# Attention scores of four 32-row heads in one PSUM tile, in place of two zero-padded pairs

## The chip, the cores and the metric

The kernel runs on one core of one Trainium2 chip. The metric is the device time of one execution in microseconds (us). Engines are named as the profile names them: PE is TensorE (PEld its weight loads), ACT is ScalarE, DVE is VectorE, POOL is GpSimd. Matmuls write into PSUM buffers; "FFN" is the feed-forward half of the block, "PV" the product of probabilities and values.

## The reference

One transformer block with its whole backward pass: 2048 positions, width 448, 16 heads of 28 channels, FFN width 1792, bf16.

```python
xn = layernorm(x)
q, k, v = split_heads(xn @ wqkv)                        # 16 heads of 28
p = softmax(einsum("bhqd,bhkd->bhqk", q, k) * 28**-0.5)
A = merge_heads(einsum("bhqk,bhkd->bhqd", p, v)) @ wo
B = (silu(xn @ w_gate) * (xn @ w_up)) @ w_down
out = x + A + B
# outputs: out, and the gradients of x, wqkv, wo, w_gate, w_up, w_down for a given grad_out
```

## The kernel before

A head's 28 channels are padded to 32 rows, so that four heads fill the 128 partitions; G = 4 such groups. For the score matmuls the kernel keeps a second copy of Q and K in DRAM (`PAIR_d`) in which a head occupies 64 rows, 32 of them zeros. Two heads lie in the two 64-row halves of PE and run side by side. Their scores form one tile of two PSUM banks, and two such tiles are in flight. Forward FFN units and weight-gradient units (`pfe`) are woven into the same loop, so that PE has other work while ACT computes exponentials.

```python
ps_u = pf.enter_context(tc.tile_pool(name="pf_psu", bufs=2, space=PSUM))   # FFN banks
...
ework = p3.enter_context(tc.tile_pool(name="p3_e", bufs=5))
ps_s = p3.enter_context(tc.tile_pool(name="p3_pss", bufs=2, space=PSUM))   # 2 tiles of 2 banks
ps_o = p3.enter_context(tc.tile_pool(name="p3_pso", bufs=1, space=PSUM))
ps_t = p3.enter_context(tc.tile_pool(name="p3_pst", bufs=1, space=PSUM))
for g in range(G):
    ...                                              # loads of qk (PAIR_d) and Vsp
    for qc in range(4):                              # 512 queries
        for kt in range(NT):                         # 16 blocks of 128 keys: 256 turns in all
            eTs = []
            for hp in range(2):
                s_ps = ps_s.tile([P, 2, 512], FP32, name="s_ps")
                for j in range(2):
                    nc.tensor.matmul(s_ps[:, j, :],
                        lhsT=KT2[hp][64*j:64*(j+1), kt*P:(kt+1)*P],
                        rhs=QT2[hp][64*j:64*(j+1), qsl],
                        start=True, stop=True, tile_position=(64*j, 0))
                eT = ework.tile([P, 2, 512], BF16, name="eT")
                nc.scalar.activation(out=eT[:], in_=s_ps[:], func=ACT.Exp, scale=SCALE)
                eTs.append(eT)
            if prev is not None:
                pv_quad(*prev)                       # four PV matmuls of the turn before
            prev = (kt, eTs)
            ...                                      # 56 ffn_unit and up to 168 pfe_unit over 256 turns
```

One weight-gradient step goes from PE to DVE and back to PE:

```python
pt = ps_u.tile([P, 4, P], BF16, name="ffn_ps")
for j in range(4):
    nc.tensor.transpose(pt[:, j, :], srcT[:, t*P:(t+1)*P], ident_bf[:])    # t = t4*4 + j
sp = ewk.tile([P, 4, P], BF16, name="ffn_sp")
nc.vector.tensor_copy(out=sp[:], in_=pt[:])
acc_ps = ps_u.tile([P, 512], FP32, name="ffn_ps")
for j in range(4):
    nc.tensor.matmul(acc_ps[:], lhsT=sp[:, j, :], rhs=rhs_sp[:, t, :], start=(j == 0), stop=(j == 3))
```

The builder sorts each engine's instructions again, so the order on PE is not that of the source; but once built it is fixed.

The softmax here doesn't subtract the row's maximum and nothing guards it: scores larger than these inputs give would overflow.

## Time and profile before

| | before |
|---|---|
| time, median of the first 3 runs | 2243 us (2233 to 2254) |
| first score matmul at | 118.8 us |
| attention forward, first score to last PV | 727 us, mean granted clock 0.96, PE busy 648 |
| tail, last PV to first output matmul | 166 us |
| output, attention backward, last gradients | 1237 us |

The lines that carry this stand in the prediction, whose forward and tail are cut within 1.1 us of these landmarks. Two more, from the page's list of costly groups (line, engine, operation, tiles, shapes, count, busy us, mean ns of one, idle before it and its main releaser):

```profile
L377 ACT ACTIVATE eT<-s_ps 128x1024 bf16<-128x1024 f32 x512 | 494.2, 1026 | 183.5 <-PE s_ps L372 170.1
L372 PE MATMUL s_ps<-qk 64*128 64x512 bf16 x1024 | 207.9, 389 | 38.8 <-ACT eT L377 32.2
```

The exponentials keep ACT busy for 494 us and the 1024 score matmuls PE for 208. ACT waits long for PE and PE briefly for ACT, so PE is the fuller of the two.

### The profile page before, as it was taken

Reading aid. Unit: us, or ns where it says so; the run is one execution under the profiler, and the core shown is the slowest. Engines: PE = TensorE matmul, PEld = TensorE weight load, DVE = VectorE, ACT = ScalarE, POOL = GpSimd, SP = SyncE. Lnnn points to the kernel's source line nnn. Section 1 sums busy time; section 2 is a strip of 40 time slices with the busy share of each in tenths; the row PEclk is TensorE's granted clock in tenths of the full one; section 3 lists DMA queues with packets and bytes.
Section 4 is the critical chain, followed back from the end, with each engine's and each line's share of the span. In section 5 each row is a group of like instructions: output and inputs, shape, how many; then the busy total and the mean of one; then the engine's idle time right before and its main releaser. Section 6 shows DMA issues by size and latency. Waiting matters only on the chain.

```text
span 2249.0 us, 30338 instructions
## 1 busy us (share of the span) xinstructions
PE 1827.5 (81%) x11579; PEld 685.4 (30%) x11672; DVE 1404.1 (62%) x2141; ACT 1086.5 (48%) x1167; POOL 25.9 (1%) x19
## 2 busy tenths in 40 slices
PE   3779989979989996569728888888888888875998
PEld 2433333333333332224302222222222222223554
DVE  4545546555555555532728788889798888874344
ACT  2167757757767770000016566656566666650100
POOL 2000000000000000000000000000000000001000
PEclk9999989989989998759858788879699979887999
DMA  5931131131121111152198887887887888787263
GB/s 200 292 110 61 63 110 61 63 109 63 55 106 63 47 46 49 61 189 95 36 338 178 155 166 170 169 164 166 158 173 164 165 171 174 150 157 229 88 202 110
DMA packets 658009, 299.56 MB, mean 133 GB/s; under 512 B 568072, under 2 KB 632712, under 8 KB 654792
## 3 DMA queue, kind: packets, MB, share of 16 engines
q1 hardware_dynamic: 632256, 252.16, 46.2%
q10 hardware_dynamic: 25608, 45.46, 6.2%
q8 instruction: 92, 1.51, 0.3%
q14 instruction: 53, 0.43, 0.1%
HBM read 99.74 MB, written 63.57 MB: 73 GB/s over the span
## 4 chain that ended last, share of the span: by engine, by line
PE 55%; DMA 18%; DVE 11%; ACT 10%; issue 5%; SPq 0%; ACTq 0%; another core or an unknown queue 0%; DVEq 0%
DMA dsT<-ds_sb 8%; PE ffn_ps L295 8%; PE dq_ps L601 7%; PE s_ps L372 5%; ACT e_sb L549 5%; PE sd_ps L530 4%; ACT eT L377 4%; DVE ds_sb L557 4%; PE o_ps L359 4%; PE sd_ps L541 4%; PE acc L572 3%; DMA srcT<-hT_d 2%; PE ffn_ps L235 2%; PE g_ps L726 2%; PE g_ps L724 2%
## 5 line engine op out<-in xcount | busy, mean ns | idle before, releaser
L557 DVE TENSOR_TENSOR ds_sb<-sd_ps,e_sb 128x1024 bf16<-128x1024 f32 x512 | 611.1, 1220 | 133.4 <-ACT e_sb L549 40.0
L549 ACT ACTIVATE e_sb<-sd_ps 128x1024 bf16<-128x1024 f32 x512 | 510.4, 1022 | 362.5 <-PE sd_ps L541 243.0
L377 ACT ACTIVATE eT<-s_ps 128x1024 bf16<-128x1024 f32 x512 | 494.2, 1026 | 183.5 <-PE s_ps L372 170.1
L530 PE MATMUL sd_ps<-bw_all 32*128 32x512 bf16 x1024 | 224.3, 431 | 57.1 <-DVE ds_sb L557 20.9
L601 PE MATMUL dq_ps<-dsT,sp_all 128*32 128x512 bf16 x1024 | 211.4, 464 | 71.6 <-DMA dsT<-ds_sb 56.3
L541 PE MATMUL sd_ps<-bw_all 32*128 32x512 bf16 x1024 | 225.0, 430 | 48.0 <-ACT e_sb L549 42.5
L372 PE MATMUL s_ps<-qk 64*128 64x512 bf16 x1024 | 207.9, 389 | 38.8 <-ACT eT L377 32.2
L572 PE MATMUL acc<-e_sb,sp_all 128*32 128x512 bf16 x1024 | 233.8, 442 | 0.3 <-DVE dkv_all L586 0.2
L579 PE MATMUL acc<-ds_sb,sp_all 128*32 128x512 bf16 x1024 | 230.0, 443 | 0.9 <-DVE ds_sb L557 0.9
L359 PE MATMUL o_ps<-eT,Vsp 128*32 128x512 bf16 x1024 | 166.8, 392 | 4.5 <-ACT eT L377 3.5
L295 PE MATMUL ffn_ps<-xn_sp,ffn_sp 128*128 128x512 bf16 x411 | 123.7, 421 | 22.3 <-DVE ffn_sp L291 18.0
L530 PEld LDWEIGHTS <-bw_all 32*128 32x128 bf16 x1024 | 57.5, 93 | 252.1 <-issue 245.9
L300 DVE TENSOR_TENSOR dwacc<-ffn_ps,dwacc 128x512 f32<-128x512 f32 x84 | 58.1, 691 | 119.3 <-PE ffn_ps L295 119.3
L541 PEld LDWEIGHTS <-bw_all 32*128 32x128 bf16 x1024 | 76.1, 93 | 148.0 <-issue 141.8
L601 PEld LDWEIGHTS <-sp_all 128*32 128x32 bf16 x1024 | 62.1, 107 | 148.1 <-issue 117.8
L291 DVE COPY ffn_sp<-ffn_ps 128x512 bf16<-128x512 bf16 x168 | 70.1, 417 | 52.6 <-PE ffn_ps L289 51.5
L372 PEld LDWEIGHTS <-qk 64*128 64x128 bf16 x1024 | 56.1, 93 | 143.9 <-issue 128.7
L289 PE MATMUL ffn_ps<-ident_bf,srcT 128*128 128x128 bf16 x672 | 73.8, 239 | 31.7 <-DMA srcT<-hT_d 17.6
L238 ACT ACTIVATE t_sb<-ffn_ps 128x512 f32<-128x512 f32 x56 | 33.5, 598 | 134.6 <-PE ffn_ps L235 134.4
L295 PEld LDWEIGHTS <-ffn_sp 128*128 128x128 bf16 x672 | 56.5, 104 | 122.8 <-DVE ffn_sp L291 59.0
L609 DVE TENSOR_TENSOR dq_acc<-dq_ps,dq_acc 64x512 f32<-64x512 f32 x96 | 65.9, 686 | 34.2 <-PE dq_ps L601 32.8
L726 PE MATMUL g_ps<-wuT_sb,duT_c 128*128 128x448 bf16 x224 | 80.1, 357 | 3.7 <-DMA duT_c<-duT_d 3.7
(137 smaller groups left out, 1886.3 us busy)
## 6 DMA issues: line engine op xcount, KB each, us to landing
qk<-PAIR_d SPq DMA_DIRECT2D x8, 1024.0 KB
dsT<-ds_sb SPq DMA_TRANSPOSE x512
hT_d<-hT SPq DMA_DIRECT2D x14, 512.0 KB
duT_d<-duT SPq DMA_DIRECT2D x14, 512.0 KB
srcT<-hT_d SPq DMA_DIRECT2D x14, 512.0 KB
daT_d<-daT SPq DMA_DIRECT2D x14, 512.0 KB
srcT<-daT_d SPq DMA_DIRECT2D x14, 512.0 KB
srcT<-duT_d SPq DMA_DIRECT2D x14, 512.0 KB
```

The lines of the kernel that those rows point to most:

```text
L295: nc.tensor.matmul(acc_ps[:], lhsT=sp[:, j, :], rhs=rhs_sp[:, t, :], start=(j == 0), stop=(j == 3))
L359: nc.tensor.matmul(o_ps[HP * hh:HP * (hh + 1), :], lhsT=Vsp[:, kt, HP * hh:HP * (hh + 1)], rhs=eTs[hp][:, j, :], start=(kt == 0), stop=(kt ...
L372: nc.tensor.matmul(s_ps[:, j, :], lhsT=KT2[hp][64 * j:64 * (j + 1), kt * P:(kt + 1) * P], rhs=QT2[hp][64 * j:64 * (j + 1), qsl], start=Tru ...
L377: nc.scalar.activation(out=eT[:], in_=s_ps[:], func=ACT.Exp, scale=SCALE)
L530: nc.tensor.matmul(s_ps[:, j, :], lhsT=QD[HP * j:HP * (j + 1), qt * P:(qt + 1) * P], rhs=KV[HP * j:HP * (j + 1), ksl], start=True, stop=Tr ...
L541: nc.tensor.matmul(dp_ps[:, j, :], lhsT=QD[64 + HP * j:64 + HP * (j + 1), qt * P:(qt + 1) * P], rhs=KV[64 + HP * j:64 + HP * (j + 1), ksl] ...
L549: nc.scalar.activation(out=e_sb[:], in_=s_ps[:], func=ACT.Exp, scale=SCALE)
L557: nc.vector.tensor_tensor(out=ds_sb[:], in0=dp_ps[:], in1=e_sb[:], op=ALU.mult)
L572: nc.tensor.matmul(acc[HP * j:HP * (j + 1), :], lhsT=dOlsp[:, qt, HP * hh:HP * (hh + 1)], rhs=e_sb[:, j, :], start=(qt == 0), stop=(qt == ...
L579: nc.tensor.matmul(acc[64 + HP * j:64 + HP * (j + 1), :], lhsT=Qsp[:, qt, HP * hh:HP * (hh + 1)], rhs=ds_sb[:, j, :], start=(qt == 0), sto ...
L601: nc.tensor.matmul(dq_ps[HP * hh:HP * (hh + 1), :], lhsT=Ksp[:, kc * 4 + kt, HP * hh:HP * (hh + 1)], rhs=dsT[:, j, kt, :], start=(kt == 0) ...
L726: nc.tensor.matmul(g_ps[:, :D], lhsT=duT_c[:, fc, tsl], rhs=wuT_sb[:, fc, :], start=(i == 0), stop=(i == n_mm - 1)); i += 1
```

## The change

The intent: four heads of 32 rows need no zero padding, four score matmuls run side by side in place of two and two, the padded copy of Q and K (and 16 stores of zeros) goes, and one exponential covers four heads. The score tile grows to four banks, so only one fits where two of two banks stood.

```diff
-    PAIR_d = dram.tile([G, 2, P, 2, S], BF16)
+    QK32_d = dram.tile([G, P, 2, S], BF16)
...                                       (memset of a zero tile and 16 stores of it removed)
-                    for hh in range(4):
-                        nc.sync.dma_start(out=PAIR_d[g, hh // 2, 64 * (hh % 2):64 * (hh % 2) + 32, tq, :],
-                                          in_=xT[HP * hh:HP * (hh + 1), :])
+                    nc.sync.dma_start(out=QK32_d[g, :, tq, :], in_=xT[:])
...
-        ework = p3.enter_context(tc.tile_pool(name="p3_e", bufs=5))
+        ework = p3.enter_context(tc.tile_pool(name="p3_e", bufs=3))
-        ps_s = p3.enter_context(tc.tile_pool(name="p3_pss", bufs=2, space=PSUM))
+        ps_s = p3.enter_context(tc.tile_pool(name="p3_pss", bufs=1, space=PSUM))
...                                       (two loads of 1 MB a group become one; pv_quad reads eT[:, hh, :])
-                    for hp in range(2):
-                        s_ps = ps_s.tile([P, 2, 512], FP32, name="s_ps")
-                        for j in range(2):
-                            nc.tensor.matmul(s_ps[:, j, :],
-                                             lhsT=KT2[hp][64 * j:64 * (j + 1), kt * P:(kt + 1) * P],
-                                             rhs=QT2[hp][64 * j:64 * (j + 1), qsl],
-                                             start=True, stop=True, tile_position=(64 * j, 0))
-                        eT = ework.tile([P, 2, 512], BF16, name="eT")
-                        nc.scalar.activation(out=eT[:], in_=s_ps[:], func=ACT.Exp, scale=SCALE)
-                        eTs.append(eT)
+                    s_ps = ps_s.tile([P, 4, 512], FP32, name="s_ps")
+                    for hh in range(4):
+                        nc.tensor.matmul(s_ps[:, hh, :],
+                                         lhsT=KT[HP * hh:HP * (hh + 1), kt * P:(kt + 1) * P],
+                                         rhs=QT[HP * hh:HP * (hh + 1), qsl],
+                                         start=True, stop=True, tile_position=(HP * hh, 0))
+                    eTs = ework.tile([P, 4, 512], BF16, name="eT")
+                    nc.scalar.activation(out=eTs[:], in_=s_ps[:], func=ACT.Exp, scale=SCALE)
```

More of the change, by code (lines that the diff above doesn't have):

```diff
@@ L82 @@
     nc.vector.memset(eps_t[:], EPS)
-    with tc.tile_pool(name="zpool", bufs=1) as zpool:
-        ztile = zpool.tile([P, 2, S], BF16)
-        nc.gpsimd.memset(ztile[:], 0.0)
-        for g in range(G):
-            for hp in range(2):
-                eng = nc.sync if (g + hp) % 2 == 0 else nc.scalar
-                eng.dma_start(out=PAIR_d[g, hp, 32:64], in_=ztile[32:64])
-                eng.dma_start(out=PAIR_d[g, hp, 96:128], in_=ztile[96:128])
     xn_sp = persist.tile([P, NT, DP_], BF16)
@@ L342 @@
         for g in range(G):
-            QT2, KT2 = [], []
-            for hp in range(2):
-                qk = inp.tile([P, 2, S], BF16, name=f"qk{hp}")
-                nc.sync.dma_start(out=qk[:], in_=PAIR_d[g, hp])
-                QT2.append(qk[:, 0, :])
-                KT2.append(qk[:, 1, :])
+            qk = inp.tile([P, 2, S], BF16, name="qk")
+            nc.sync.dma_start(out=qk[:], in_=QK32_d[g])
+            QT, KT = qk[:, 0, :], qk[:, 1, :]
             Vsp = inp.tile([P, NT, P], BF16, name="Vsp")
@@ L353, with pv_quad @@
                 o_ps = ps_o.tile([P, 512], FP32, name="o_ps")
-                def pv_quad(kt, eTs):
-                    for hp in range(2):
-                        for j in range(2):
-                            hh = 2 * hp + j
-                            nc.tensor.matmul(o_ps[HP * hh:HP * (hh + 1), :],
-                                             lhsT=Vsp[:, kt, HP * hh:HP * (hh + 1)],
-                                             rhs=eTs[hp][:, j, :],
-                                             start=(kt == 0), stop=(kt == NT - 1),
-                                             tile_position=(0, HP * hh),
-                                             skip_group_check=True)
+                def pv_quad(kt, eT):
+                    for hh in range(4):
+                        nc.tensor.matmul(o_ps[HP * hh:HP * (hh + 1), :],
+                                         lhsT=Vsp[:, kt, HP * hh:HP * (hh + 1)],
+                                         rhs=eT[:, hh, :],
+                                         start=(kt == 0), stop=(kt == NT - 1),
+                                         tile_position=(0, HP * hh),
+                                         skip_group_check=True)
@@ L366 @@
                 prev = None
                 for kt in range(NT):
-                    eTs = []
-                    for hp in range(2):
-                        s_ps = ps_s.tile([P, 2, 512], FP32, name="s_ps")
-                        for j in range(2):
-                            nc.tensor.matmul(s_ps[:, j, :],
-                                             lhsT=KT2[hp][64 * j:64 * (j + 1), kt * P:(kt + 1) * P],
-                                             rhs=QT2[hp][64 * j:64 * (j + 1), qsl],
-                                             start=True, stop=True, tile_position=(64 * j, 0))
-                        eT = ework.tile([P, 2, 512], BF16, name="eT")
-                        nc.scalar.activation(out=eT[:], in_=s_ps[:], func=ACT.Exp, scale=SCALE)
-                        eTs.append(eT)
+                    s_ps = ps_s.tile([P, 4, 512], FP32, name="s_ps")
@@ new lines @@
+                    for hh in range(4):
+                        nc.tensor.matmul(s_ps[:, hh, :],
[4 more added lines that the diff above has]
+                    nc.scalar.activation(out=eTs[:], in_=s_ps[:], func=ACT.Exp, scale=SCALE)
```

## The prediction

> **What bounds the kernel now.** I read the busy rows over 40 slices of the page first, then the busy time of each engine in six stretches that I cut at landmarks of the timeline, then the waits and the timeline inside the stretches that the change touches.
>
> The busy tenths in 40 slices:
>
> ```profile
> PE   3779989979989996569728888888888888875998
> ACT  2167757757767770000016566656566666650100
> PEclk9999989989989998759858788879699979887999
> DMA  5931131131121111152198887887887888787263
> ```
>
> ScalarE (ACT) works in slices 2 to 15 and again from slice 21 on: the attention forward and the attention backward. The diff touches only the first of these, and the projection stage ahead of it. Between them lies a stretch where ACT is at 0 and the granted clock sinks to 0.5. The stretches in numbers (PE, weight load, VectorE, ACT, GpSimd busy us, clock, DMA share, GB/s):
>
> ```profile
> 0.00:118.80 118.80, 66.78 (x514) 40.30 (x523) 62.87 (x151) 19.74 (x34) 14.04 (x14) 1.00 0.78 250
> 118.80:846.50 727.70, 648.10 (x3809) 245.35 (x3875) 402.73 (x771) 522.60 (x561) 3.12 (x2) 0.96 0.21 72
> 846.50:1011.00 164.50, 107.49 (x434) 45.00 (x441) 78.49 (x144) 4.78 (x8) 0.00 (x0) 0.69 0.29 99
> ```
>
> The first is loads and projections (DMA 78% busy), the second the attention forward with the FFN woven into it (PE 89% busy, ACT 72%), the third a tail: FFN work that did not fit beside the attention, at a mean clock of 0.69. The rest (1238 us) is output, attention backward and last gradients.
>
> Inside the forward, the waits:
>
> ```profile
> ACT eT L377 <- PE s_ps L372: 170.1, 209, 11.1
> PE s_ps L372 <- ACT eT L377: 32.2, 101, 1.0
> ```
>
> ACT waits for scores 170 us, PE for the exponentials only 32 us: mostly PE's turn order bounds the forward. The PE timeline shows what a turn costs (start, duration):
>
> ```profile
> 150.37 0.39 PE L372 MATMUL s_ps<-qk 64*128 64x512 bf16 x2
> 150.69 0.39 PE L359 MATMUL o_ps<-eT,Vsp 128*32 128x512 bf16 x2
> 151.01 0.39 PE L372 MATMUL s_ps<-qk 64*128 64x512 bf16 x2
> ...
> 152.92 0.61 PE L372 MATMUL s_ps<-qk 64*128 64x512 bf16 x4
> 153.45 0.40 PE L359 MATMUL o_ps<-eT,Vsp 128*32 128x512 bf16 x4
> ...
> 154.49 0.39 PE L372 MATMUL s_ps<-qk 64*128 64x512 bf16 x2 [0.63 <-ACT eT L377]
> ```
>
> Starts are 0.32 us apart for a pair of score matmuls and equally for a pair of PV matmuls; four scores take 0.53, because only two run beside each other. So one streaming of 512 columns is 0.53-0.32 = 0.21 us, and each change of matmul kind adds about 0.11 us. In the tail one weight-gradient step looks so:
>
> ```profile
> 989.07 1.89 PE L295 MATMUL ffn_ps<-xn_sp,ffn_sp 128*128 128x512 bf16 x4 [0.69 <-DVE ffn_sp L291]
> 990.75 0.63 PE L289 MATMUL ffn_ps<-ident_bf,srcT 128*128 128x128 bf16 x4
> 992.07 1.89 PE L295 MATMUL ffn_ps<-xn_sp,ffn_sp 128*128 128x512 bf16 x4 [0.69 <-DVE ffn_sp L291]
> ```
>
> It takes 3.0 us there, at half clock and in a chain through VectorE, against about 1.3 us of PE time when it is woven into the forward (four matmuls of 0.215, four transposes of 0.06, two entries).
>
> **What the Trainium skill says.** "TensorEngine Tiling (Array Packing)", section Key Properties: a change of tiling mode drains TensorE. The 0.11 us above agree. "TensorE: Matmul & The Clock Gate", section Part 3: Packing small matmuls, The mechanism: row tiles run concurrently with starts about 4 ns apart; the trace agrees for pairs, and a quad of PV column tiles passes in 153.78-153.45 = 0.33 us, so I take four 32-row tiles as 0.32 us. Same page, Part 1: the clock falls to half after an idle window of about 3.4 us; the trace shows 0.5 in the tail. "ScalarE: Activation LUTs", What ACT_TABLE_LOAD costs: 0.833 ns per element plus a fixed part. The trace gives 1.026 us for 1024 columns and 0.598 us for 512, so 0.836 ns a column.
>
> **The change part by part.**
>
> Startup. The GpSimd memset of the zero tile (3.51 us in the timeline) and 16 zero stores of 256 KB (4.2 MB) go. The chain of the first 23 us is one load:
>
> ```profile
> 1.25 21.71 DMA x_sb<-in_A_x_dram
> ```
>
> From 4 to 24 us the queues move 350 to 396 GB/s at a share of 1.0, so this load shares saturated engines with the zeros. Without them x, dy and the QKV weights (4.9 MB) at about 360 GB/s should be in by 15 to 16 us: 7 us less, carried on through statistics and transposes. The projections (56 to 118 us) write as many bytes as before, 1.5 MB in each 5.5 us, at a DMA share of 0.9 and more, so I expect nothing from the fewer, larger stores. The first score load is 1 MB instead of 2 MB: at about 300 GB/s 3.5 us earlier. Startup: -11 us.
>
> Forward, PE time. I listed PE's instruction order in both built kernels. The builder re-sorts work, so the diff alone does not tell this. Before, the stretch from first score to last PV has 1131 changes of matmul kind; after, 948. Score groups go from 447 to 321 and PV groups from 404 to 302. With 0.215 us a streamed group, 0.10 a change and 0.08 more on entering FFN matmuls, I added up before at 635 us of pure PE work: scores 123, PV 90, FFN and transposes 287, changes 136. Measured are 728 us, so 93 us are waits. After: scores 69, PV 66, changes 121, FFN and transposes 334: 590 us. That is 45 us less although the order now holds 300 more FFN matmuls in this stretch (before 1720 of them, after 2020).
>
> Forward, the new chain. The score buffer is the same four banks, but one tile of four heads instead of two tiles of two. Scores of the next key block cannot start until the whole exponential has been read. One turn of this chain is: scores to start of exponential 0.49 us (152.92 to 153.41 on the timeline), an exponential over 2048 columns 1.026+1024*0.836 ns = 1.88 us, back to PE 0.06 us: 2.43 us. 256 turns are 622 us by themselves. PE's order is fixed, so turns do not average out: those with little work wait for the chain, those with much stretch it. Also in 61 of 256 turns the order puts FFN matmuls between the scores of one quad, so the exponential waits for them (86 us in all). Taking each turn as the larger of its PE work and 2.43 us, plus what splits its quad, I get 726 us, with about 140 us of PE idle.
>
> To this come waits that the tally leaves out. Of the 93 us before, 36 were for exponentials and are replaced. I keep about 12 us at the start for the FFN weights (a 10 us load on the chain at 124 us), 20 us for VectorE copies, 12 us for three changes of head group (one 1 MB load each, where before two loads collided with FFN stores and ACT stood still for up to 11.1 us), and allow little for spells of half clock. Forward: about 775 us, +47.
>
> Tail. What the forward takes in leaves the tail. Before, after the last PV there are 36 weight-gradient steps and 8 whole FFN units. After, 12 steps and the last third of one unit remain, that is the last FFN block alone. Before, that very block took from its store at 966.3 us to 1011, 45 us; with a few us to finish the unit I take 50 us against 164.5. Tail: -114 us.
>
> From there on the instruction order is the same row for row on PE (13,873 rows), so nothing else moves. Sum: 2243 - 11 + 47 - 114 = 2165 us; I choose 2162, since some allowances overlap.
>
> **The rivals.**
> (a) The chain wins outright: the single score tile makes every light turn 2.43 us, and PE, idle more often, falls to half clock, after which heavy turns get longer too. For it: two turns in a row with only scores and PV occur about a dozen times (0.65 us work in 2.43), and PE fell to 0.5 at idle spells around 294 and 477 us. Against it: at half clock a turn fills with PE work, and the clock came back within 15 us before. It would make the forward 820 us or more and the total about 2210, within 2%.
> (b) PE work is what counts and the waits overlap: forward about 700 us (590 plus some 110), total near 2090. For it: PE waited only 32 us for exponentials before. Against it: that was with two score tiles in flight.
> (c) The expected gain is only the removed packing: the forward follows its PE time, but the FFN is bound by VectorE, so the tail returns as VectorE waits inside. VectorE was busy 403 of 728 us; moving in 24 steps (1.1 us each) and 8 units (4.8 us each) gives 468 of 775, 60%. It does not bind on average; locally it can cost 20 us more.
> (d) The load from the new score buffer or its stores shows: 4 loads of 1 MB, hidden but for a few us at four places. Under 10 us either way.
>
> **Range and chances.** The tail's fall is the surest term, since it follows from the order (10 us either way); the startup is good to 5 us; the forward may err by 45 us either way. Runs before spread over 2233 to 2254. So 2162 us, eight in ten between 2098 and 2215. Faster by over 2% means below 2198: 0.81. Within 2%: 0.17. Slower: 0.02.
>
> **What would show it.** In the profile after: an exponential of about 1.88 us, 256 times; PE waiting for it over 100 us, where it was 32; ACT waiting less than 170 us for scores; the tail with ACT at 0 shrinking from three slices to about one (50 us); the x load landing at 16 us; the first score matmul near 108 us. Wrong I would be if four 32-row score matmuls do not start together (a quad then takes 0.5 us or more), if the clock in the forward falls below 0.85, or if the tail stays over 100 us.

## The result, and the profile after

The changed kernel is correct and takes 2271 us (median of 12 runs, 2263 to 2296) against 2254 us for the kernel before (15 runs, 2233 to 2274). The ratio is 1.0096 with a 95% interval of 1.006 to 1.013: about 1% slower, which is "within 2%". (Ratios are the mean time of one kernel's fast runs over that of the other's in the same rounds, so not quite the ratio of the medians quoted.) The prediction was 2162, with a range of 2098 to 2215.

The first profile fell on the slowest of the 12 runs (2296 us) and lacks some matmul records. So I had the same kernel profiled once more (e9 below, 2276 us); the forward took 876 us in both. Its stages against those of before, in us:

| stage | before | changed (e9) | difference | predicted |
|---|---|---|---|---|
| up to the first score | 118.8 | 113.5 | -5.3 | -11 |
| forward | 727.4 | 876.0 | +148.6 | +47 |
| tail | 165.9 | 44.2 | -121.7 | -114 |
| output, backward, last gradients | 1236.9 | 1241.0 | +4.1 | 0 |
| span | 2249.0 | 2274.7 | +25.7 | -78 |

(The first profile's backward took 891 us; before has 868, e9 879, and experiments that do not touch it 870 to 888. That is the spread from run to run.)

The busy tenths in 40 slices of the changed kernel, from its page:

```profile
PE   3877877777777777778728888888888888875998
ACT  2056656555555556510015565656566656650100
PEclk9978889898888889879857897779699879786999
```

Where the PE row before read mostly 9 and 8 through slices 4 to 15, it now reads 7 and 8, through slice 17. The clock row shows 8s where 9s stood. ACT stands at 0 in two slices (19 and 20), where before it did so in five (16 to 20): the tail, some three of these five, has nearly gone. The stages of e9 in numbers (stretch, length, busy us of PE, PEld, DVE, ACT, POOL with counts, clock, DMA share, GB/s):

```profile
0.00:113.50 113.50, 69.14 (x524) 41.94 (x524) 63.02 (x151) 19.68 (x34) 10.57 (x13) 0.97 0.66 215
113.50:989.50 876.00, 681.38 (x4176) 254.47 (x4175) 458.71 (x872) 510.52 (x313) 3.12 (x2) 0.87 0.19 63
989.50:1033.70 44.20, 30.34 (x150) 13.54 (x149) 20.32 (x44) 0.35 (x1) 0.00 (x0) 0.74 0.68 238
```

In the forward PE is busy for 681 us and idle for 876.0 - 681.4 = 194.6; before it was busy for 648 and idle for 80. So against before both terms grew: idle by 115 us, and busy by 34, although the score matmuls became cheaper. Part of the new busy time is the FFN work that came in from the tail; part is clock. The clock records of these traces are all full or half, so a mean of 0.87 means (1 - 0.87) x 2 x 876 = 228 us at half clock. The records themselves add up to 229 us, against 55 before.

The waits in the forward, first profile of the changed kernel (waiter, what for, us in total, times, longest):

```profile
ACT eT L359 <- PE s_ps L354: 334.5, 226, 5.8
...
PE s_ps L354 <- ACT eT L359: 57.5, 75, 1.7
...
PE ffn_ps L284 <- DVE ffn_sp L280: 45.8, 90, 0.9
PE ffn_ps L278 <- DVE negw L242: 38.2, 34, 1.8
```

ACT's wait for scores doubled, from 170 to 334 us. PE's wait for exponentials is 57 us, not the large number one would expect of a chain through the exponential. Two waits for DVE come close to that: 46 us for the copy of the transposes and 38 us for the last step of the FFN's `negw`. How the two combine is seen on the timeline (start, duration, what it waited for):

```profile
304.79 0.39 PE L354 MATMUL s_ps<-qk 32*128 32x512 bf16 x4
305.12 0.39 PE L343 MATMUL o_ps<-eT,Vsp 128*32 128x512 bf16 x1
...
307.23 0.40 PE L354 MATMUL s_ps<-qk 32*128 32x512 bf16 x4
...
307.73 1.88 ACT L359 ACTIVATE eT<-s_ps 128x2048 bf16<-128x2048 f32 x1 [0.56 <-PE s_ps L354]
...
309.24 0.38 PE L278 MATMUL ffn_ps<-ident_bf,srcT 128*128 128x128 bf16 x4 [1.28 <-DVE negw L242]
...
310.52 1.37 PE L284 MATMUL ffn_ps<-dy_sp,ffn_sp 128*128 128x512 bf16 x3 [0.90 <-DVE ffn_sp L280]
...
312.25 0.61 PE L354 MATMUL s_ps<-qk 32*128 32x512 bf16 x4
...
312.98 1.88 ACT L359 ACTIVATE eT<-s_ps 128x2048 bf16<-128x2048 f32 x1 [3.37 <-PE s_ps L354]
```

The first two lines: four 32-row matmuls pass in 305.12 - 304.79 = 0.33 us, the time of one streaming and one change of kind, as the prediction wanted. The turn at 307.23 shows what goes wrong. Next in PE's fixed order stand four transposes, which wait for DVE until 309.24. When the exponential ends at 309.61 and the score tile is free, PE stands before matmuls that wait until 310.52 for the copy of those transposes. It reaches the next scores at 312.25, and ACT has stood still for 3.37 us because no second tile was in flight. The same four score matmuls now take 0.61 us for each (0.40 before): the clock record goes to half at 310.64, after these two waits.

### The profile page after: what moved, and what is told of

It is laid out like the page before. It is cut to its first block, busy times and chain, and to the rows that moved or that the text cites.

```text
span 2294.2 us, 29778 instructions
## 1 busy us (share of the span) xinstructions
PE 1790.9 (78%) x11579; PEld 665.1 (29%) x11672; DVE 1403.0 (61%) x2141; ACT 1071.2 (47%) x911; POOL 22.4 (1%) x18
## 5 line engine op out<-in xcount | busy, mean ns | idle before, releaser
L359 ACT ACTIVATE eT<-s_ps 128x2048 bf16<-128x2048 f32 x256 | 480.5, 1877 | 337.1 <-PE s_ps L354 334.5
L511 PE MATMUL sd_ps<-bw_all 32*128 32x512 bf16 x1024 | 230.0, 443 | 55.8 <-DVE ds_sb L538 18.8
L522 PE MATMUL sd_ps<-bw_all 32*128 32x512 bf16 x1024 | 231.4, 443 | 44.4 <-ACT e_sb L530 38.8
L553 PE MATMUL acc<-e_sb,sp_all 128*32 128x512 bf16 x1024 | 238.8, 450 | 0.1
L354 PE MATMUL s_ps<-qk 32*128 32x512 bf16 x1024 | 140.6, 430 | 64.3 <-ACT eT L359 57.5
L284 PE MATMUL ffn_ps<-xn_sp,ffn_sp 128*128 128x512 bf16 x416 | 135.4, 443 | 40.7 <-DVE ffn_sp L280 37.2
L343 PE MATMUL o_ps<-eT,Vsp 128*32 128x512 bf16 x1024 | 133.3, 425 | 3.6 <-ACT eT L359 3.4
L278 PE MATMUL ffn_ps<-ident_bf,srcT 128*128 128x128 bf16 x672 | 80.6, 254 | 56.6 <-DVE negw L242 38.2
L229 DVE SCALAR_TENSOR_TENSOR g<-t_sb,ffn_ps 128x512 f32<-128x512 f32 x56 | 38.5, 687 | 88.2 <-ACT t_sb L227 88.2
L278 PEld LDWEIGHTS <-srcT 128*128 128x128 bf16 x672 | 57.7, 114 | 115.1 <-issue 83.2
L284 PE MATMUL ffn_ps<-dy_sp,ffn_sp 128*128 128x512 bf16 x203 | 75.3, 501 | 18.9 <-DVE ffn_sp L280 17.0
```

The source lines that it names most:

```text
L278: nc.tensor.transpose(pt[:, j, :], srcT[:, t * P:(t + 1) * P], ident_bf[:])
L343: nc.tensor.matmul(o_ps[HP * hh:HP * (hh + 1), :], lhsT=Vsp[:, kt, HP * hh:HP * (hh + 1)], rhs=eT[:, hh, :], start=(kt == 0), stop=(kt == ...
L354: nc.tensor.matmul(s_ps[:, hh, :], lhsT=KT[HP * hh:HP * (hh + 1), kt * P:(kt + 1) * P], rhs=QT[HP * hh:HP * (hh + 1), qsl], start=True, st ...
L359: nc.scalar.activation(out=eTs[:], in_=s_ps[:], func=ACT.Exp, scale=SCALE)
L511: nc.tensor.matmul(s_ps[:, j, :], lhsT=QD[HP * j:HP * (j + 1), qt * P:(qt + 1) * P], rhs=KV[HP * j:HP * (j + 1), ksl], start=True, stop=Tr ...
L522: nc.tensor.matmul(dp_ps[:, j, :], lhsT=QD[64 + HP * j:64 + HP * (j + 1), qt * P:(qt + 1) * P], rhs=KV[64 + HP * j:64 + HP * (j + 1), ksl] ...
```

## The experiments

Fifteen runs were made, one of them (e9) of the changed kernel itself. Unless it is said otherwise a result is correct. All stage times are from one profile each; a total with a ratio is the median of four runs, one without is a single run.

### e1 and e2: which half of the change costs the forward?

The change does two things at once: 32-row tiling and the merging of two score tiles into one. e1 keeps the 32-row tiling and goes back to two tiles; e2 is the kernel before with one merged tile.

```diff
 # e1, against the changed kernel
-        ps_s = ... bufs=1 ...;  ework bufs=3
+        ps_s = ... bufs=2 ...;  ework bufs=5
-                    s_ps = ps_s.tile([P, 4, 512], FP32, name="s_ps")
-                    for hh in range(4):
+                    for hp in range(2):
+                        s_ps = ps_s.tile([P, 2, 512], FP32, name="s_ps")
+                        for j in range(2):                 # hh = 2*hp + j, 32 rows as before; one exp per tile
 # e2, against the kernel before
-        ps_s = ... bufs=2 ...;  ework bufs=5
+        ps_s = ... bufs=1 ...;  ework bufs=3
+                    s_ps = ps_s.tile([P, 4, 512], FP32, name="s_ps")     # one tile, 64-row pairs, one exp
```

> The new layout and the 32-row tiles, but two score tiles of two heads with an exponential each, as before. Theory A (the single four-head score tile is the cause: scores of the next key block cannot run while the exponential reads, so every FFN wait at the head of PE's order also stalls ScalarE): forward back near 715 us, ACT waiting for scores under 190 us, mean clock of the forward 0.95 or more, total 2225 to 2245 with the tail long again (about 165 us). Rival B (the 32-row tiling itself slows PE or its clock): forward 850 us or more and a clock near 0.87, as in the changed kernel. Rival C (the builder pulls FFN into the forward and the two FFN banks stall PE): the order here holds as much FFN as before (1700 matmuls in the forward), so C also says near 2240; it is told apart by the run with a third FFN bank.

> The zero-padded 64-row layout of before, but one score tile of four heads and one exponential. Theory A: at least as slow as the changed kernel, forward 876 us or more (up to 256 x 0.21 = 54 us more for scores that run two at a time), total 2275 to 2330. Rival B (32-row tiling to blame): near the kernel before, 2250.

e1 took 2256 us (ratio to before 1.000, 0.992 to 1.008), e2 2281 (1.011, 1.003 to 1.019). The forward of e1, then of e2:

```profile
114.10:841.30 727.20, 670.25 (x3856) 247.39 (x3855) 394.55 (x761) 523.59 (x560) 3.12 (x2) 0.91 0.20 66
```

```profile
122.70:996.60 873.90, 698.14 (x4172) 252.50 (x4171) 458.92 (x872) 511.18 (x313) 3.12 (x2) 0.92 0.19 66
```

With two tiles the forward is 727 us, as before, and the tail 173; with one tile it is 874 and the tail 42, as in the changed kernel. So both the longer forward and the shorter tail come from the merged tile; the 32 rows move neither. Nor do they shorten the forward, as they were meant to: e1 saves one streaming of 0.21 us in each turn that keeps a quad together, yet its forward equals that of before, at a clock of 0.91 in place of 0.96. (That clock, and e1's total, are misses of theory A, which expected 0.95 or more and 2225 to 2245 us; ACT's wait for scores in e1, 168 us, is as it said.)

### e3, e4 and e5: the chain by itself

To see the chain without other work, the FFN units were taken out of the loop and left to the end. e3 is the kernel before so treated, e4 the changed one. e5 is e4 with six quads of zero-weight matmuls added to each turn: work that changes no result and only keeps PE busy.

```diff
 # e3 and e4 (the FFN's PSUM pool opens only after the loop; ps_t has 3 banks in place of 1)
-                    if (c * 56) // 256 > ((c - 1) * 56) // 256 and ffn_units:
-                        ffn_unit(*ffn_units.pop(0))
-                    ...                                    (and the pfe units)
 # e5, against e4
+                        if 0 < prev[0] < NT - 1:
+                            for _ in range(6):
+                                for hh in range(4):
+                                    nc.tensor.matmul(o_ps[HP * hh:HP * (hh + 1), :],
+                                                     lhsT=zw[:, HP * hh:HP * (hh + 1)], rhs=prev[1][:, hh, :],
+                                                     start=False, stop=False, ...)
```

> Kernel before with all FFN work moved behind the attention forward, so the forward shows its own rate. Theory A: bound by ScalarE, 512 exponentials at 0.943 us = 483 us plus about 16 x 3 us at the changes of query chunk: 520 to 540 us from first score to last PV.

> Changed kernel with all FFN work moved behind the forward. Theory A: the chain of 2.43 us a turn shows bare: 256 x 2.43 = 622 us plus 16 x 2 us, 650 us, up to 720 if the clock falls to half because PE is busy only 0.65 us of each turn. Rivals B and C predict no more than in the run of before alone (530 us), since no FFN is there and PE has slack.

> The changed kernel's attention alone (694.6 us at a mean clock of 0.50), with six extra quads of matmuls with zero weights a turn into the PV sum, which add 0 and about 1.3 us of PE work to each turn. If the chain of 2.43 us a turn at full clock is the floor and the half clock the rest: the clock rises over 0.9 and the forward falls to 640 to 660 us in spite of four times the PV work. If the clock is not what lengthens the turn (the chain is longer for another reason): the forward stays at 695 us or grows.

The forward alone took 496 us in e3 (clock 0.97; shorter than expected), 695 in e4 (0.50) and 659 in e5 (0.92), both as expected. (The totals, 2665, 2855 and 2819 us, mean nothing here, since the FFN stands behind the attention with a tail of about 790 us.) The turns, e3 first (two score groups make a turn, 2 x 0.91 us):

```profile
401.73 0.39 PE L371 MATMUL s_ps<-qk 64*128 64x512 bf16 x2 [0.20 <-ACT eT L376]
...
402.64 0.39 PE L371 MATMUL s_ps<-qk 64*128 64x512 bf16 x2 [0.20 <-ACT eT L376]
```

Two turns of e4, and its forward:

```profile
401.24 0.62 PE L353 MATMUL s_ps<-qk 32*128 32x512 bf16 x4 [1.49 <-ACT eT L358]
...
403.89 0.62 PE L353 MATMUL s_ps<-qk 32*128 32x512 bf16 x4 [1.49 <-ACT eT L358]
```

```profile
124.70:819.30 694.60, 317.25 (x2108) 88.99 (x2107) 31.14 (x135) 481.79 (x257) 0.00 (x0) 0.50 0.02 9
```

And of e5, a turn and the forward:

```profile
401.58 0.40 PE L355 MATMUL s_ps<-qk 32*128 32x512 bf16 x4 [0.41 <-ACT eT L360]
...
404.02 0.40 PE L355 MATMUL s_ps<-qk 32*128 32x512 bf16 x4 [0.41 <-ACT eT L360]
```

```profile
124.90:783.70 658.80, 522.81 (x7480) 208.93 (x7480) 30.67 (x135) 481.06 (x257) 0.00 (x0) 0.92 0.03 10
```

Two things follow. The chain is real and its size at full clock is the predicted one, 404.02 - 401.58 = 2.44 us a turn. And PE's clock stays at half through e4, by the clock records in all but the first 1.1 us of the forward. Yet PE has no long idle time in it: the usual gap is 1.49 us and the longest in the whole stretch 2.85 us. It is idle often enough. Work that computes nothing made e5 36 us shorter than e4, because at full clock the scores release the exponential earlier. Here the causal part of the clock is shown, since e5 adds only work.

### e6, e7, e8 and e12: is it the FFN's two banks, or the long exponential?

A rival said that the merged tile only lays bare a shortage of FFN banks. The transposes of the attention output (`ot_ps`) can share the FFN's pool, which frees one bank for it. e6 does so in the changed kernel, e7 in e1 (32 rows, two tiles), e12 in the kernel before (64 rows, two tiles). Another rival said that the 2048-column exponential holds the tile too long; e8 reads the one tile in two exponentials of 1024 columns.

```diff
 # e6, e7, e12
-    ps_u = ... name="pf_psu", bufs=2 ...
+    ps_u = ... name="pf_psu", bufs=3 ...
-        ps_t = p3.enter_context(tc.tile_pool(name="p3_pst", bufs=1, space=PSUM))
-                    ot_ps = ps_t.tile([P, P], FP32, name="ot_ps")
+                    ot_ps = ps_u.tile([P, P], FP32, name="ffn_ps")
 # e8, against the changed kernel (ework bufs=5)
-                    nc.scalar.activation(out=eTs[:], in_=s_ps[:], func=ACT.Exp, scale=SCALE)
+                    for hp in range(2):
+                        eT = ework.tile([P, 2, 512], BF16, name="eT")
+                        nc.scalar.activation(out=eT[:], in_=s_ps[:, 2 * hp:2 * hp + 2, :], func=ACT.Exp, scale=SCALE)
```

> The changed kernel with three PSUM banks for the FFN instead of two (the small transposes share them). Rival C (two FFN banks: PE stands at the head of its order for VectorE, 101 us of waits): these waits fall below 50 us and the forward from 876 to 800 us or less, total 2200. Theory A (the single score tile): the waits move onto the exponential instead, forward over 840 us, total within 1.5% of the changed kernel.

> 32-row tiles with two score tiles (the run that took 2256 us) and three FFN banks. Theory A: with two score tiles the attention has slack, so a third bank lets the builder take more FFN into the forward at little cost: forward about 740 us, tail 130 us or less, total 2200 to 2230, under both kernels. Rival C: the same or better, 2180. If it does not beat 2250, the FFN banks bind nothing.

> The changed kernel with its one score tile, but two exponentials of 1024 columns in place of one of 2048. Theory A (the buffer, not the size of the instruction): forward within 25 us of 876, as scores of the next block still wait for both. If the long instruction is to blame (tanh of the FFN and PV wait behind 1.88 us of exponential): forward 800 us or less.

> The kernel before (64-row pairs, two score tiles) with only the third FFN bank, no 32-row tiling. If the win of the run with 32-row tiles and three banks (2208 us) comes from the bank: 2205 to 2220 us here. If the 32-row tiles are part of it: 2230 us or more.

With one tile neither helps: e6 took 2288 us with a forward of 876 (ratio 1.016, 1.008 to 1.024), e8 2283 us with 880. Both rivals fall. With two tiles the third bank helps: e7 took 2208 us (0.982, 0.978 to 0.986) and e12 2193 us (0.971, 0.967 to 0.975), less than the 2205 to 2220 expected of it. (Whether e7 is faster by 2% is open by its interval.) The forward of e7, then of e12:

```profile
112.20:870.40 758.20, 692.54 (x4040) 266.13 (x4039) 423.89 (x821) 524.77 (x565) 3.12 (x2) 0.92 0.21 71
```

```profile
121.30:859.90 738.60, 672.16 (x4065) 267.23 (x4064) 427.78 (x833) 522.84 (x566) 3.12 (x2) 0.98 0.23 77
```

About as many matmuls as in the changed kernel's forward (4176) pass here in 739 to 758 us, not 876: PE is idle for 66 us in both, against 195. So it is not the FFN work moved in from the tail that makes the forward long, but that work with a single score tile. And e12 against e7 shows again no gain in time from the 32 rows.

### e9: the changed kernel again

> The changed kernel as it is, once more with a profile, because its first profiled run (2296 us) was the slowest of its twelve. If the 23 us that its backward was longer there (891 against 868 us) is run-to-run spread: a backward of 865 to 885 us and a total of 2265 to 2280 us here, with the forward still at 870 to 880 us.

It took 2276 us; its lines stand above. All 4176 matmuls of the forward's order are in its trace, so its busy time is the one to count with. It agrees with the first profile on forward (876 us) and clock (0.87).

### e10 and e13: one wait for VectorE taken away

Here the weight-gradient matmuls read the untransposed `srcT`, so they no longer wait for the copy. The copy still runs. The three FFN weight gradients come out wrong (relative error 1.41); nothing else does. e10 does this to the changed kernel, e13 to the kernel before.

```diff
-            nc.tensor.matmul(acc_ps[:], lhsT=sp[:, j, :], rhs=rhs_sp[:, t, :],
+            nc.tensor.matmul(acc_ps[:], lhsT=srcT[:, t * P:(t + 1) * P], rhs=rhs_sp[:, t, :],
```

> Wrong result on purpose: the weight-gradient matmuls of the changed kernel read the loaded block itself, not the copy that VectorE makes of its transpose; transposes and copies still run, so the work is the same, only PE's wait for that copy (46 us before matmuls, 83 us before their weight loads) is gone. Theory A in its full form (in a turn PE has nothing to run beside the FFN, so each wait for VectorE delays the next scores): forward down from 876 to 790 us or less. If the half clock or the chain of scores and exponential is what counts: forward 850 us or more.

> Control for the run of the changed kernel without the copy wait: the same edit in the kernel before (wrong result on purpose). There PE waited only 5 us in matmuls and 28 us in weight loads for that copy. If such waits cost a forward with two score tiles little because PE has scores to run meanwhile: forward plus tail down by 15 to 45 us at most, with the builder taking more FFN into the forward, and PE's waits for VectorE in the forward under 20 us. If the edit is simply cheaper everywhere: forward plus tail down by as much as in the changed kernel (51 us) or more.

The forward of e10, then of e13:

```profile
111.10:949.70 838.60, 646.66 (x4180) 253.35 (x4179) 461.42 (x876) 510.05 (x313) 3.12 (x2) 0.89 0.19 65
```

```profile
117.50:867.60 750.10, 699.11 (x4158) 268.86 (x4157) 457.62 (x869) 529.28 (x568) 3.12 (x2) 0.99 0.23 77
```

e10 took 2226 us; its forward of 839 lies between what the two theories expected, a miss for both. e13 took 2154 us. Its first alternative (15 to 45 us at most) missed and its second held: forward and tail together lost 104 us, more than the 48 that the same edit took off the changed kernel (forward 876 to 839, tail 44 to 34). So the wait for the copy is not peculiar to the single tile. The use of the pair is another one: now both forwards hold nearly the same matmuls (4180 and 4158) and lack the same wait, and they take 839 and 750 us. PE is idle for 192 us in the one and 51 in the other. In e10 PE's idle time hardly changed against e9 (195 to 192 us), although the copy wait is gone; what fell is its busy time (681 to 647), and with it the half-clock time, from 229 to 178 us. So the wait taken away came back as other waits.

### e11 and e14: filling the changed kernel

The zero-weight quads of e5, in the changed kernel with its FFN: two a turn in e11, one in e14.

```diff
+                            for _ in range(2):             # 1 in e14
+                                ... four zero-weight matmuls into o_ps, as in e5
```

> The changed kernel with two extra quads of zero-weight matmuls a turn (about 0.43 us of PE work each turn, 110 us in all at full clock), to hold the clock up beside the FFN. If half clock (0.87 on average in the forward) is the main part of the 101 us missed: clock over 0.95 and a forward no longer than 876 us in spite of the added work. If waits for VectorE and turn order are the main part: forward longer, 900 to 960 us, whatever the clock does.

> The changed kernel with one extra zero-weight quad a turn (48 us of PE work at full clock in all; two of them gave a clock of 0.95 and a forward of 895 us). If the half clock costs the forward tens of us: clock 0.90 to 0.93 and a forward of 865 to 880 us, that is the added 48 us cost nothing. If it costs next to nothing: 885 us or more.

e14 took 2281 us with a forward of 880 at clock 0.90, at the upper end of what was expected if half clock costs tens of us. e11 took 2294 us with 895 at 0.95, between its two theories and a miss for both. One quad is 0.21 us, in 224 of the 256 turns: 47 us of added work cost the forward 3.5 us, and 94 us cost 19. Part of the fill goes into idle time (PE idle 195, 162, 146 us in e9, e14, e11), part is paid back by the clock (229, 171, 96 us at half clock). A filler is not a repair, then, but it confirms that PE has room that its work does not use, and that filling it lifts the clock.

### e15: a version that beats both

e12 with the FFN units started a little earlier in the loop:

```diff
-                    if (c * 56) // 256 > ((c - 1) * 56) // 256 and ffn_units:
+                    if (c * 68) // 256 > ((c - 1) * 68) // 256 and ffn_units:
-                    n_pfe = (c * 168) // 256 - ((c - 1) * 168) // 256
+                    n_pfe = (c * 210) // 256 - ((c - 1) * 210) // 256
```

> The best version so far (64-row pairs, two score tiles, three FFN banks, 2193 us) with the FFN handed out a fifth faster, so that it ends inside the forward: 98 more FFN matmuls... in the builder's order 2116 instead of 1912 of them lie in the forward. If PE has room there: tail 87 to about 45 us, forward 739 to 770 us, total 2170 to 2195. If the work only changes place, as in the changed kernel: within 1% of 2193.

```profile
117.00:912.40 795.40, 705.54 (x4266) 283.39 (x4265) 462.94 (x886) 523.93 (x569) 3.12 (x2) 0.98 0.26 87
```

It took 2168 us (ratio 0.962, 0.955 to 0.969). The forward takes in nearly all the FFN work, 4266 matmuls, in 795 us at a clock of 0.98, and a tail of 10 us is left. (More moved than expected, so forward and tail lie outside the figures expected, and the total just under.) This is what the change was predicted to bring, reached with 64-row pairs, two tiles and a third FFN bank.

## Why the prediction was wrong

Point by point:

- **Startup** (-11): -5.3. The zeros did go, but the x load ended DVE's wait at 19.9 us, not at 15 to 16: in the first 25 us the queues moved 6.9 MB, not the 4.9 reckoned with, since more weight loads share them (those of `wo` and `w_down` are in the list of issues there).
- **Four 32-row matmuls in one streaming, an exponential of 1.88 us, a chain of 2.43 us a turn**: right. The trace has 0.33 us a quad, 256 exponentials of 1877 ns, and e5 a turn of 2.44.
- **Tail** (-114, to 50 us): right, 44 us.
- **Nothing after it moves**: +4 us, within the spread of the backward.
- **Forward** (+47, to 775 us): this failed, measured 876. The prediction's sum was 590 us of PE work and 185 us of waits: 140 idle in the chain, and 12 + 20 + 12 = 44 for weights, VectorE copies and loads. Measured are 681 us busy and 195 idle. That the waits agree as a total is luck. In e9 PE waited only 59 us for exponentials:

```profile
PE s_ps L354 <- ACT eT L359: 55.9, 72, 1.7
...
PE o_ps L343 <- ACT eT L359: 3.4, 2, 1.7
```

The other 135 us, where the prediction had 44, it waited for the rest, above all for VectorE (46 and 38 us in the first profile's lines, where the prediction had 20). ACT waited longer for scores, not less. The timeline at 307 us shows the swap: PE spends the exponential's time, and more, standing before DVE's results.

- **Two terms of the forward were mis-sized: the 44 us for waits other than those for exponentials, and "allow little for spells of half clock".** The first measured 135 us. For the second: the PE work came out at 681 in place of 590, 91 us more. At half clock PE was busy for 192 of the 229 us (from the trace's clock records; from the views alone, 228 us at the forward's busy share of 0.78 give 178). Half of that is time that full clock would not have taken: 96 us by the trace, 89 by the views. So 681 - 96 = 585 us: the tally of 590 holds at full clock. The same for before: 648 us less some 19 for its 55 us at half clock, against a tally of 635.
- **What each of the two cost** can be estimated from e9's trace in the prediction's own terms, turn by turn from exponential to exponential. The larger of 2.43 us and the turn's PE work at full clock (busy time less half of that at half clock) adds up to 686 us (714 if the turns are cut at the exponentials' ends, not their starts). With the stretch by half clock added to the work it is 754 us (791), with PE's waits other than for exponentials added instead 782 (774), with both 865 (858), against 876 measured. So in this estimate half clock cost 68 to 84 us, and those waits 60 to 111. The prediction's own figure for the turns, 726 us, was above both, which hid part of the miss.

The prediction's rival (a) had named the clock: the chain makes PE idle, the clock halves, the forward is 820 us or more. I set it aside since "at half clock a turn fills with PE work, and the clock came back". That argument was wrong. In e4 the turn does not fill (317 us busy of 695, at 0.50 throughout), and with the FFN woven in PE stands before DVE and ACT in so many turns that the clock falls again and again. The reading that I lacked is in "TensorE: Matmul & The Clock Gate", Part 1, section A second HAM failure mode: psum-queue depth-cycling, where short idles between groups of matmuls, through PSUM buffers taken in turn, make the clock swing. The trace of the kernel before had a hint of it too: its clock went to half at 292.8 and 477.1 us, when PE's longest single wait in the 10 us before was 1.8 and 1.5 us. I had taken only the idle window of about 3.4 us from that page, and looked for long gaps. e4 agrees with the section in kind: gaps of 1.49 us, at most 2.85, were enough to keep it down. The prediction's own warning threshold, a forward clock below 0.85, was set without working out what it is worth. The clock of 0.87 passed it, and went with about 90 us of stretched work.

Shown, then: the merged tile makes the forward long (e1 against the changed kernel, e2 against before, e10 against e13); the FFN's banks and the length of the exponential do not (e6, e8); and a starved PE runs at half clock, where added work can shorten it (e4 to e5). By accounting, the 101 us missing in the forward are 91 of work stretched by the clock and 10 of waits, but such a sum does not say what caused what. With one score tile the time at half clock ran from 143 us (e8) and 147 (e2) over 229 (e9) to 259 (e6) by the clock records, and the forward was 874 to 880 us in all four; in e2 and e8 more PE work (639 and 657 us at full clock, against 585 in e9) stood in the place of the stretch. How much a full clock alone would have given back stays open: in e11 and e14 half-clock time and idle time fell together, and e10 took away a wait and lost half-clock time with hardly any idle time.

Open, too, is why the 32-row tiling brought no gain. In all three pairs that differ in it, the 32-row kernel had the lower forward clock: 0.91 in e1 against 0.96 before, 0.87 in the changed kernel against 0.92 in e2, 0.92 in e7 against 0.98 in e12. The forwards of the pairs are level or longer (727 and 727, 876 and 874, 758 and 739 us), so the saved streaming, up to 256 x 0.21 = 54 us, does not show in the time. It does show in PE's work, if half of the busy time at half clock is taken off: 585 us in the changed kernel against 639 in e2, 606 in e1 against 629 before, 637 in e7 against 663 in e12. Half clock and waits took it back. That a PE with shorter work idles more, and so falls to half clock more often, would fit, but no run isolates it; and e8, with 32 rows and one tile, had 0.92.

## What to carry to other kernels

Merging two buffered tiles into one turns an overlap into a chain, even if the bytes and the banks stay the same; with a fixed instruction order every wait of the feeding engine then stops the fed engine too. When a change makes PE idle more often, price the clock: with a clock that is only full or half, as in these traces, time at half clock is (1 - mean clock) x 2 x the stretch, and up to half of the busy time in it is lost. An agreeing total of waits is no check either: compare them by what PE waits for. Work moved out of the tail was gained here only where two score tiles stayed in flight: one more FFN bank with two score tiles gave 3% (e12), and earlier FFN units nearly one more (e15).

## What the Trainium skill lacked or had wrong

- "TensorE: Matmul & The Clock Gate", Why this matters for your kernels: its rule is that no idle gap should pass about 3 us. It is not enough. e4 stayed at half clock for all but the first 1.1 of its 695 us with gaps of 1.49 us in turns of 2.65, the longest gap being 2.85; e5 reached 0.92 with more work in the turn. The same page, A second HAM failure mode, speaks of a clock that swings; in e4 it stayed down.
- The same page gives no busy share at which the clock comes back. PE was busy for 192 of its 229 us at half clock in the changed kernel (84%), where the clock came and went, and for 317 of 694 us in e4 (46%), where it never came back; no run here isolates the share.
- "TensorEngine Tiling (Array Packing)", Key Properties: the drain at a change of mode has no figure there. Here it is about 0.11 us at full clock (0.32 us from group to group, of which 0.21 is streaming).
- No page speaks of row tiling and the granted clock together. In three pairs the kernel with 32 rows had the lower clock in the forward: 0.91 against 0.96 with 64, 0.87 against 0.92, 0.92 against 0.98. The cause is open (e8, 32 rows too, had 0.92).
